# One pool of eight PSUM banks for scores and PV sums, with order rules chosen anew, in a fused attention and feed-forward kernel

## The chip, the cores and the metric

The kernel runs on one core of a Trainium2 chip. The metric is the device time of one execution in microseconds (us). Most executions agree within 0.3%. An execution can also fall into a slower state, with a lower granted clock; one did (experiment 10), and it is left out: fast executions are compared with fast ones only.

## The reference

```
xn  = layernorm(x)                         # x: 1 x 2048 x 640, bfloat16
q   = xn @ wq  -> 32 heads of 20           # wq: 640 x 640
k, v = xn @ wk, xn @ wv                    # ONE head of keys and values, 20 wide
p   = softmax(q k^T / sqrt(20))            # 32 heads x 2048 x 2048
att = (p v) @ wo
h   = relu(xn @ w1 + b1) ** 2              # 640 -> 1536
out = x + att + h @ w2 + b2
```

The scores are 2048 tiles of 128 keys x 512 queries. Each needs an exponential and a product with the values; the rest is small beside that.

## The kernel before

The program is not written as a fixed order. A list scheduler in it plans all instructions with modelled durations, picks a PSUM bank for each product, and then emits one instruction list per engine. What matters here:

- **Two ways for a tile.** ScalarE takes exponentials of two or three neighbouring banks at once (1480 tiles). VectorE and GpSimd replace the exponential of the other 568 by an approximation: four tiles (one VectorE score *set*) are evicted by VectorE as integers, then shifted in three *passes*.
- **Blocks.** 32 blocks of four heads x 512 queries. All PV products of a block (values times probabilities) add up in one bank. Then VectorE copies the sum out.
- **Banks.** PSUM is the memory that TensorE's products land in; the program has it as eight banks of 512 columns. A product is *evicted* when another engine copies it out. Seven banks are a pool for scores and dense products; the eighth belongs to the PV sums.
- **Start.** Rows are normalised, transposed and projected in four quarters. Scores of a quarter of keys can begin when that quarter has left PSUM (`KTe`).
- **Rules.** A table gives the scheduler other priorities in each stretch of 10 us of its plan.

```python
NB = 7          # pool: banks 0 to 6
PVB = 7         # the PV sums' own bank
RULES = {3: {'PVA': 2.1, 'PVD': 2.1, 'R3': 1, 'PP': 0.9}, ...}     # ... cut
ACTST = (2, 5, 6)             # rows with statistics on ScalarE

def make_step():                                   # scores for one exponential
    ...
    st_of = {bk: bank_state(bk) for bk in range(NB)}
    ...                                            # three neighbours, or the pair that is free first
        can = sorted((max(st_of[bk], st_of[bk + 1], t0), bk) for bk in range(NB - 1)
                     if st_of[bk] is not None and st_of[bk + 1] is not None)

def make_pv(b, kt):                                # PV products of block b
    first, last = b not in pv_begun, pv_count[b] == KT - 1
    ...
        parts.append(mm(ps[32 * h:32 * h + 32, PVB, :], vx[:, kt, :], PT[:, sl, :], first, last, (0, 32 * h)))
    if first and b > 0:
        deps.append(tn_op[b - 1])                  # wait until the old sum has been copied

def warm_parts():                                  # filler at the start
    return [lambda e: e.matmul(ps[:, PVB, :], ones_bf[:, :], hT_tmp[:, 0, :], start=True, stop=True)]

def odma(st, evs):                                 # store of a finished row block, by SyncE
    dma_out[st] = op(f"OD{st}", "SP", 0.45, lambda e: e.dma_start(out[0, st * 128:(st + 1) * 128, :], orow(st)), evs, ...)
```

The softmax here doesn't subtract the row's maximum and nothing guards it: scores larger than these inputs give would overflow.

## Time and profile before

| | before |
|---|---|
| time | 705.43 us, median of 3 (705.3 to 706.33) |
| profiled run | 705.39 us, span 703.6 |
| busy: TensorE, ScalarE, VectorE, GpSimd | 99%, 98%, 92%, 61% |
| exponentials that ScalarE issues | 715 (1480 tiles) |
| exponential that waits for the third quarter of keys | 32.44 us |
| last exponential ends | 695.14 us |
| last copy out by VectorE ends | 701.17 us |

The prediction below shows how the page, the chain and the start are read. Two more places also belong here. The first is the fourth quarter of keys, in VectorE's timeline (columns: start, length of the group, engine, line, operation, output and input, count, and in brackets the idle time before it and what ended it):

```profile
35.13 0.75 DVE L554 TENSOR_SCALAR kT<-ps,nk 128x512 bf16<-128x512 f32 x1 [1.80 <-PE ps L367]
```

The second is SyncE's issue of the four output stores at the end. Three issues take 1.30 us in all, and the last one is made 0.16 us after VectorE's last copy (701.17):

```profile
699.98 1.30 SPq L708 DMA_DIRECT2D out_dram<-out_sb  x3
701.33 0.45 SPq L708 DMA_DIRECT2D out_dram<-PT  x1
```

### The profile page before, as it was taken

How to read it: one execution, taken by the hardware profiler on the slowest of the kernel's cores; microseconds unless marked ns; L12 is line 12 of the kernel's file. 1: busy time of each engine (PE TensorE's matmuls, PEld its weight loads, DVE VectorE, ACT ScalarE, POOL GpSimd, SP SyncE). 2: the span in 40 equal slices, each digit the busy share in tenths (PEclk: the TensorE clock that was granted, in tenths of full speed). 3: DMA queues.
4: the chain of work that ended last, by engine and by line, in shares of the span. 5: the costliest groups of instructions: out<-in, count | busy, mean ns of one | idle time of the engine just before them, and what ended most of it. 6: DMA issues, size and time to landing. Idle time of an engine off the chain costs nothing.

```text
span 703.6 us, 22608 instructions
## 1 busy us (share of the span) xinstructions
PE 695.0 (99%) x9780; PEld 216.0 (31%) x9781; DVE 645.9 (92%) x1125; ACT 687.5 (98%) x739; POOL 427.3 (61%) x268
## 2 busy tenths in 40 slices
PE   8999999999999999999999999999999999999997
PEld 4422223233322223332322222323333222233333
DVE  7789999999999998989998998899899999999894
ACT  6899999999999999999999999999999999999995
POOL 4767556567566764666568765766665675644253
PEclk9999999999999999999999999999999999999999
DMA  6325422233337701211101001111112100031201
GB/s 201 98 70 153 115 78 58 81 97 80 84 85 160 162 20 25 55 40 37 52 18 40 23 22 28 29 47 26 46 42 51 36 22 23 20 106 51 55 26 39
DMA packets 42016, 44.00 MB, mean 63 GB/s; under 512 B 15540, under 2 KB 32772, under 8 KB 41788
## 3 DMA queue, kind: packets, MB, share of 16 engines
q1 hardware_dynamic: 39132, 36.93, 19.2%
q0 software_dynamic: 2208, 5.25, 3.9%
q8 instruction: 76, 1.25, 0.7%
q10 hardware_dynamic: 576, 0.38, 0.2%
q14 instruction: 24, 0.20, 0.1%
HBM read 28.03 MB, written 14.91 MB: 61 GB/s over the span
## 4 chain that ended last, share of the span: by engine, by line
ACT 95%; PE 4%; DMA 1%; DVE 0%; SPq 0%; issue 0%; DVEq 0%
ACT PT L910 94%; PE ps L367 3%; DMA x_sb<-in_A_x_dram 1%; PE ps L540 1%; ACT xnT L477 0%; ACT OC L421 0%; DVE out_sb L1164 0%; PE ps L568 0%; SPq L384 0%; ACT OC L422 0%; SPq L391 0%; PE ps L510 0%; PE ps L496 0%; DVEq L227 0%; DVE PT L1164 0%
## 5 line engine op out<-in xcount | busy, mean ns | idle before, releaser
L910 ACT ACTIVATE PT<-ps 128x1024 bf16<-128x1024 f32 (+1 forms) x715 | 677.1, 1219 | 3.8 <-PE ps L367 3.8
L1083 DVE TENSOR_SCALAR tmore<-ps 128x512 uint16<-128x512 f32 x568 | 367.4, 683 | 31.7 <-PE ps L367 28.2
L1101 POOL TENSOR_SCALAR tmore<-tmore 128x2048 uint16<-128x2048 uint16 x109 | 206.4, 1900 | 171.1 <-PE ps L367 62.3
L367 PE MATMUL ps<-qT,kT 20*128 20x512 bf16 x2048 | 281.7, 384 | 1.9 <-ACT PT L910 0.8
L1101 POOL TENSOR_SCALAR x_sb<-tmore 128x2048 uint16<-128x2048 uint16 x100 | 189.3, 1902 | 79.4 <-DVE x_sb L1101 24.2
L367 PEld LDWEIGHTS ps<-qT,kT 20*128 20x128 bf16 x2048 | 71.6, 91 | 280.4 <-ACT PT L910 233.1
L367 PE MATMUL ps<-PT,vx 128*32 128x512 bf16 x1480 | 136.9, 386 | 0.2 <-ACT PT L910 0.2
L1101 DVE TENSOR_SCALAR x_sb<-tmore 128x2048 uint16<-128x2048 uint16 x135 | 96.1, 745 | 0.1
L367 PE MATMUL ps<-x_sb,vxs 128*32 128x512 bf16 x940 | 83.2, 382 | 0.0
L367 PE MATMUL ps<-xnT,w_sb 128*32 128x512 bf16 x960 | 77.2, 384 | 0.1
L367 PE MATMUL ps<-w_sb,big 128*32 128x320 bf16 x1536 | 74.5, 302 | 0.0
L367 PE MATMUL ps<-tmore,vxs 128*32 128x512 bf16 x764 | 69.6, 382 | 0.0
L1101 DVE TENSOR_SCALAR tmore<-tmore 128x2048 uint16<-128x2048 uint16 x82 | 61.5, 770 | 0.1
L367 PE MATMUL ps<-tmore,vx 128*32 128x512 bf16 x568 | 55.7, 382 | 0.0
L367 PEld LDWEIGHTS ps<-PT,vx 128*32 128x32 bf16 x1480 | 34.9, 94 | 62.1 <-issue 53.6
L367 PEld LDWEIGHTS ps<-w_sb,big 128*32 128x32 bf16 x1536 | 32.1, 95 | 29.3 <-issue 22.2
L648 DVE TENSOR_SCALAR hT_tmp<-ps,b1col 128x512 bf16<-128x512 f32 x48 | 35.8, 746 | 3.4 <-PE ps L367 2.7
L367 PE MATMUL ps<-xnT,wq_sb 128*32 128x512 bf16 (+1 forms) x480 | 33.7, 356 | 0.2 <-DVE tmore L1083 0.2
L367 PE MATMUL ps<-wo_c,OC 128*32 128x320 bf16 x608 | 30.9, 301 | 0.0
L367 PEld LDWEIGHTS ps<-x_sb,vxs 128*32 128x32 bf16 x940 | 21.3, 95 | 19.9 <-issue 13.4
L367 PEld LDWEIGHTS ps<-xnT,w_sb 128*32 128x32 bf16 x960 | 17.6, 94 | 26.7 <-issue 22.4
L367 PEld LDWEIGHTS ps<-tmore,vxs 128*32 128x32 bf16 x764 | 18.1, 95 | 16.4 <-issue 11.5
(81 smaller groups left out, 259.4 us busy)
## 6 DMA issues: line engine op xcount, KB each, us to landing
xbd<-b2d SPq DMA_DIRECT2D x16, 320.0 KB, 4.4
xbd<-in_A_x_dram POOLq DMA_DIRECT2D x8, 640.0 KB, 5.8
xr<-xbd SPq DMA_DIRECT2D x32, 160.0 KB, 2.4
w_sb<-in_B_w_dram SPq DMA_DIRECT2D x8, 480.0 KB, 4.4
big<-OR SPq DMA_DIRECT2D x71, 40.0 KB
big<-drs SPq DMA_DIRECT2D x71, 40.0 KB
out_dram<-out_sb SPq DMA_DIRECT2D x15, 160.0 KB, 1.8
qT<-QCr SPq DMA_DIRECT2D x108, 20.0 KB
```

The costliest lines, as they stand in the source:

```text
L367: return lambda e: e.matmul(out_, l, r, start=start, stop=stop, tile_position=tp)
L540: return [(lambda e, dt=dt: e.transpose(out=psbf(bk)[:, dt * 128:(dt + 1) * 128], in_=xn_sb[:, st, dt:D:DT], identity=ident[:])) for dt in ...
L648: o = Op(f"RL{qc}_{f}", "DVE", 0.66, [lambda e: e.tensor_scalar(out=hT_tmp[:, k % 2, :], in0=ps[:, bk, :], scalar1=b1col[:, f:f + 1], scal ...
L910: return Op(f"ACT{st_['j']}", "ACT", 0.05 + 0.4267 * n, [lambda e: e.activation(out=PT[:, s0:s0 + n, :], in_=ps[:, b0:b0 + (n - 1) * db + ...
L1083: d1 = op(f"D1_{n}_{i}", "DVE", 0.60, lambda e: e.tensor_scalar(out=L[:, cs].bitcast(U16), in0=ps[:, bank, :], scalar1=XA, scalar2=XB, op0 ...
L1101: p = op(f"P{j}_{n}", eng, 0.60 if eng == "DVE" else 1.86, lambda e, T=T, j=j, two=two: e.tensor_scalar(out=T.bitcast(U16), in0=L.bitcast( ...
```

## The change

The intent: let the PV sum take any free bank. The next block's sum can then begin while VectorE still has to copy the old one, and the scores can use the eighth bank when it is free. The order rules were chosen again for this scheduler, with more weight on VectorE score sets early in each stretch.

```diff
-NB = 7
-PVB = 7
+NB = 8
+PV0 = 7
-RULES = {3: {'PVA': 2.1, 'PVD': 2.1, 'R3': 1, 'PP': 0.9}, ...      (the whole table, 51 entries: cut)
+DJIT = 9.0
+RULES = {3: {'D1P': 0.5, 'R3': 1}, 4: {'BEHIND': -0.1, 'PVA': 2.1}, ...      (cut)
-QEACT = (0, 1, 2, 3)
+QEACT = (0, 1)                       # two of four query evictions go to VectorE
-ACTST = (2, 5, 6)
-POOLXN = (2, 7, 9, 10, 11, 13, 14, 15)
+ACTST = (0, 2, 4)
+POOLXN = (7, 9, 10, 11, 13, 14, 15)
 ...                                   # PRIO, NBEF and FFN0 have other values too: cut
 def make_step():
-            st_of = {bk: bank_state(bk) for bk in range(NB)}
+            keep = kept()             # one bank is kept for a sum about to begin
+            st_of = {bk: bank_state(bk) if bk != keep else None for bk in range(NB)}
 ...
+        def bank_for(b):
+            if b in pv_bank:
+                return pv_bank[b]
+            can = [(bank_state(bk), -bk) for bk in range(NB) if bank_state(bk) is not None and ...]
+            return -min(can)[1] if can else None
 ...
 def make_pv(b, kt):
-                parts.append(mm(ps[32 * h:32 * h + 32, PVB, :], ...))
-            if first and b > 0:
-                deps.append(tn_op[b - 1])
+                parts.append(mm(ps[32 * h:32 * h + 32, bank, :], ...))
+            if first:
+                deps.append(bank_rel[bank])
 ...
 def make_dqk(heads):                  # scores for VectorE
+            if max(free["DVE"], free["PE"]) + sum(...) > free["PE"] + 0.43 + par("DJIT"):
+                return None
```

More of the change, by code (lines that the diff above doesn't have):

```diff
@@ L80 @@
 KEEP = 1
-RULES = {3: {'PVA': 2.1, 'PVD': 2.1, 'R3': 1, 'PP': 0.9},
-         4: {'PVA': 2.1, 'PVD': 2.1, 'R3': 1, 'PP': 0.9, 'WARM': 0.78},
-         5: {'D1P': 1, 'MPRIO': 0.5, 'PBIAS': 2.5},
-         6: {'D1P': 1, 'MPRIO': 0.5, 'PBIAS': 2.5, 'ND': 1, 'QKP': 0},
-         7: {'DQP': 2.05, 'URG': 2, 'PVD': 2.1, 'BEHIND': -0.3},
-         8: {'WARM': 0.85, 'DQP': 0.95},
-         10: {'ND': 1, 'NOPEN': 3},
-         11: {'ND': 1, 'NOPEN': 3},
-         12: {'EPS': 0.12},
-         13: {'EPS': 0.06, 'EVP': 0.3},
-         15: {'PBIAS': 0},
-         17: {'EPS': 0.06},
-         18: {'EPS': 0.12},
-         19: {'WARM': 0.78, 'PBIAS': 2.5, 'IDLE': 0.3},
-         21: {'PBIAS': 0, 'KEEP': 0},
-         23: {'EPS': 0.12},
-         25: {'R3': 1, 'EVP': 0.3},
-         26: {'R3': 1, 'EVP': 0.3, 'IDLE': 0.3, 'PVD': 2.1},
-         28: {'EPS': 0.12, 'URG': 3},
-         29: {'EPS': 0.12, 'URG': 3, 'KEEP': 3, 'EVP': 1.1, 'ND': 3},
-         31: {'PBIAS': 1, 'D1P': 1, 'PVD': 1.05},
-         32: {'PBIAS': 1, 'D1P': 1, 'PVD': 1.05, 'DGAP': 0.8, 'DQP': 0.95, 'SQP': 2, 'R3': 1},
-         36: {'PP': 0.9, 'BEHIND': -0.1, 'EVP': 0.3, 'PBIAS': 1.5},
-         37: {'URG': 3, 'JIT': 1.0, 'PVD': 1},
-         38: {'SQP': 0.7, 'URG': 3},
-         39: {'PP': 2.5},
-         40: {'PBIAS': 1},
-         41: {'PBIAS': 1, 'DGAP': 1.5, 'SQP': 0.7},
-         42: {'PBIAS': 1, 'DGAP': 1.5, 'SQP': 2, 'NOPEN': 3, 'ND': 2, 'PVD': 1},
-         43: {'PBIAS': 1, 'DGAP': 1.5, 'SQP': 2, 'NOPEN': 3, 'ND': 2, 'PVD': 1, 'R3': 9},
-         44: {'WARM': 0.78, 'KEEP': 3, 'DLAST': 7.5},
-         45: {'DGAP': 0.8, 'KEEP': 1, 'D1P': 3},
-         48: {'PBIAS': 1},
-         49: {'PBIAS': 1, 'R3': 1},
-         50: {'PBIAS': 1, 'R3': 1},
-         53: {'DLAST': 3.5},
-         54: {'DLAST': 3.5, 'EPS': 0, 'EVP': 0.3},
-         55: {'DLAST': 3.5, 'EPS': 0, 'EVP': 0.3, 'ND': 1},
-         56: {'EVP': 2, 'MPRIO': 1.0},
-         57: {'R3': 1, 'ND': 1},
-         58: {'BEHIND': -0.1, 'EPS': 0, 'PP': 4, 'R3': 1},
-         59: {'BEHIND': -0.1, 'EPS': 0, 'PP': 4, 'R3': 1, 'DRATE': 0.95, 'DLAST': 10, 'PVA': 2.1},
-         60: {'EVP': 1.1},
-         61: {'EVP': 1.1, 'SQP': 0.7},
-         62: {'EVP': 1.1, 'SQP': 0.7, 'KEEP': 3, 'R3': 1, 'NOPEN': 2, 'D1P': 3},
-         64: {'PP': 0.9, 'DRATE': 0.8},
-         65: {'R3': 1},
-         66: {'R3': 1},
-         67: {'EPS': 0.12, 'PVA': 1.05},
-         68: {'R3': 0},
-         69: {'R3': 0, 'JIT': 1.1}}
@@ new lines @@
+DJIT = 9.0
+RULES = {3: {'D1P': 0.5, 'R3': 1},
+         4: {'BEHIND': -0.1, 'PVA': 2.1},
+         6: {'EPS': 0.06},
+         7: {'EPS': 0.06, 'D1P': 0.5, 'KEEP': 1},
+         9: {'PBIAS': 1, 'PVA': 1, 'IDLE': 0.2, 'EPS': 0},
+         10: {'PBIAS': 1, 'PVA': 1, 'IDLE': 0.2, 'EPS': 0, 'ND': 1, 'NOPEN': 3},
+         11: {'IDLE': 2, 'EPS': 0.06},
+         13: {'URG': 3, 'KEEP': 3, 'NOPEN': 2, 'MPRIO': 0.9},
+         14: {'DRATE': 0.95, 'PBIAS': 0},
+         15: {'EPS': 0},
+         16: {'EPS': 0, 'KEEP': 0, 'DJIT': 9, 'PBIAS': 2.5},
+         17: {'MPRIO': 0.9, 'ND': 1},
+         18: {'MPRIO': 0.9, 'ND': 1, 'PBIAS': 1.5},
+         19: {'DLAST': 3.5, 'D1P': 3},
+         20: {'DLAST': 3.5, 'D1P': 3, 'PP': 2.5, 'PVD': 1.05},
+         21: {'DLAST': 3.5, 'D1P': 3, 'PP': 2.5, 'PVD': 1.05, 'DJIT': 0.6},
+         22: {'PP': 2.5, 'SQP': 0.7, 'BEHIND': 0.25},
+         23: {'PP': 2.5, 'SQP': 1.5, 'BEHIND': 0.25},
+         26: {'PVD': 2.1, 'EVP': 2, 'BEHIND': -0.1, 'DQP': 0.95},
+         27: {'QKP': 0, 'JIT': 1.1},
+         28: {'QKP': 0, 'JIT': 1.1, 'EVP': 2, 'R3': 0},
+         30: {'MPRIO': 1.0},
+         31: {'D1P': 0.5},
+         32: {'D1P': 0.5, 'DRATE': 1.1},
+         35: {'PP': 2.5, 'JIT': 0.9},
+         36: {'PP': 2.5, 'JIT': 0.9, 'DGAP': 0.8, 'URG': 3},
+         37: {'PBIAS': 1},
+         38: {'PBIAS': 1},
+         39: {'PBIAS': 1, 'MPRIO': 0.9, 'KEEP': 2, 'EPS': 0.06},
+         40: {'PBIAS': 1, 'MPRIO': 0.9, 'KEEP': 2, 'EPS': 0.06, 'R3': 0},
+         42: {'D1P': 3},
+         43: {'DJIT': 1.0, 'EVP': 0.3, 'PBIAS': 2.5},
+         44: {'URG': 4, 'PVA': 1.05, 'JIT': 0.82},
+         45: {'URG': 4, 'PVA': 1, 'JIT': 0.82, 'R3': 1, 'DLAST': 10, 'PBIAS': 2.5},
+         46: {'URG': 4, 'PVA': 1, 'JIT': 1.1, 'R3': 1, 'DLAST': 10, 'PBIAS': 2.5, 'EVP': 0.8, 'ND': 1, 'SQP': 0.7},
+         47: {'URG': 4, 'PVA': 1, 'JIT': 1.1, 'R3': 1, 'DLAST': 10, 'PBIAS': 2.5, 'EVP': 0.8, 'ND': 1, 'SQP': 0.7, 'DJIT': 0.6, 'EPS': 0.06},
+         51: {'QKP': 0, 'KEEP': 3},
+         52: {'DRATE': 0.95, 'PP': 4, 'MPRIO': 1.0, 'R3': 1},
+         54: {'PBIAS': 1.5, 'JIT': 1.0, 'IDLE': 0.1},
+         55: {'PBIAS': 1.5, 'JIT': 1.0, 'IDLE': 0.1, 'URG': 4, 'D1P': 0.5, 'EPS': 0.06},
+         56: {'PVA': 1.05, 'PBIAS': 0.6},
+         57: {'PBIAS': 1, 'DGAP': 1.5, 'KEEP': 2},
+         58: {'PBIAS': 0, 'DGAP': 1.5, 'KEEP': 2, 'R3': 1},
+         59: {'DRATE': 1.1},
+         60: {'DRATE': 1.1, 'PP': 2.5},
+         62: {'IDLE': 2, 'R3': 0},
+         63: {'PVD': 2.1},
+         64: {'JIT': 0.9, 'PBIAS': 0.6, 'SQP': 1.5, 'R3': 0},
+         65: {'PBIAS': 1.5},
+         66: {'PBIAS': 1.5, 'PP': 4, 'DQP': 2.05, 'SQP': 0.7, 'R3': 0},
+         68: {'EVP': 0.3, 'PVA': 1.05},
+         69: {'R3': 1}}
@@ L132 @@
 HOOK = None
-PRIO = {'NM15': 2.12, 'NM10': 2.88, 'PW2': 0.96}
-NBEF = {'AG4': 10.21, 'NM7': 11.5, 'Qe0_1': 10.11, 'PW12': 25.33}
+PRIO = {'XN1': 0.13}
+NBEF = {'S4a': 6.0, 'AG5': 10.23, 'PW1': 4.94}
 XACT = (1, 3)
-QEACT = (0, 1, 2, 3)
+QEACT = (0, 1)
 STOP = None
@@ L143 @@
 EARLYK = "F"
-FFN0 = 0.3
+FFN0 = 0.6
 OUT0 = 0.5
@@ L159 @@
 DEFAULTS = dict(EVP=EVP, PBIAS=PBIAS, MPRIO=MPRIO, DGAP=DGAP, DLAST=DLAST, DRATE=DRATE, BEHIND=BEHIND, IDLE=IDLE, URG=URG, NOPEN=NOPEN,
-                EPS=0.03, JIT=JIT, R3=R3, STATIC=STATIC, PVA=1, PVD=1, D1P=1, PP=4, SQP=2, DQP=3, QKP=0, ND=2, WARM=WARM, KEEP=KEEP)
+                EPS=0.03, JIT=JIT, R3=R3, STATIC=STATIC, PVA=1, PVD=1, D1P=1, PP=4, SQP=2, DQP=3, QKP=0, ND=2, WARM=WARM, KEEP=KEEP, DJIT=DJIT)
 class Ctr:
@@ L506, in fill_parts @@
         def fill_parts():
-            return [mm(ps[32 * jj:32 * jj + 32, PVB, :], zeros32[:, :], kT[:, 0:512], False, False, (0, 32 * jj)) for jj in range(4)]
+            return [mm(ps[32 * jj:32 * jj + 32, pv_bank[pv_blk[0]], :], zeros32[:, :], kT[:, 0:512], False, False, (0, 32 * jj)) for jj in range(4)]
         def warm_parts():
-            return [lambda e: e.matmul(ps[:, PVB, :], ones_bf[:, :], hT_tmp[:, 0, :], start=True, stop=True)]
+            return [lambda e: e.matmul(ps[:, PV0, :], ones_bf[:, :], hT_tmp[:, 0, :], start=True, stop=True)]
         def need_te(sts):
@@ L920, in after_act, with kept, pv_begin @@
                     pv_ready[key[0]].append(("A", key[1]))
+        pv_bank = {0: PV0}
+        bank_busy[PV0] = True
+        def bank_for(b):
+            if b in pv_bank:
+                return pv_bank[b]
+            can = [(bank_state(bk), -bk) for bk in range(NB) if bank_state(bk) is not None and not (par("STATIC") and bk in HELD)]
+            return -min(can)[1] if can else None
+        def kept():
+            b = pv_blk[0]
+            return bank_for(b) if b < NBLK and b not in pv_begun else None
+        def pv_begin(b):
+            if b not in pv_begun:
+                pv_bank[b] = bank_for(b)
+                bank_busy[pv_bank[b]] = True
+                pv_begun.add(b)
         def make_pv(b, kt):
@@ L924, in make_pv @@
             parts, deps = [], []
+            bank = bank_for(b)
             for h in range(HPG):
@@ L927, in make_pv @@
                 deps.append(o)
-                parts.append(mm(ps[32 * h:32 * h + 32, PVB, :], vx[:, kt, :], PT[:, sl, :], first, last, (0, 32 * h)))
+                parts.append(mm(ps[32 * h:32 * h + 32, bank, :], vx[:, kt, :], PT[:, sl, :], first, last, (0, 32 * h)))
             deps.append(v_op[kt // 4])
-            if first and b > 0:
-                deps.append(tn_op[b - 1])
+            if first:
+                deps.append(bank_rel[bank])
             return Op(f"PV{b}_{kt}", "PE", 0.222, parts, deps)
@@ L939, in make_dpv @@
             parts = []
+            bank = bank_for(b)
             for h in range(HPG):
                 i = s["order"].index(h)
-                parts.append(mm(ps[32 * h:32 * h + 32, PVB, :], wgt[:, kt, :], src[:, i * 512:(i + 1) * 512], first, last, (0, 32 * h)))
+                parts.append(mm(ps[32 * h:32 * h + 32, bank, :], wgt[:, kt, :], src[:, i * 512:(i + 1) * 512], first, last, (0, 32 * h)))
             deps.append(v_op[kt // 4])
@@ L945, in make_dpv @@
                 deps.append(vs_op[kt // 4][term - 1])
-            if first and b > 0:
-                deps.append(tn_op[b - 1])
+            if first:
+                deps.append(bank_rel[bank])
             return Op(f"DPV{b}_{kt}_{term}", "PE", 0.2205, parts, deps)
@@ L966, in emit_norm @@
             a = b % NOR
+            pb = pv_bank[b]
             if b >= NBLK - 2:
                 Tn, T2 = OR[:, a, :], QCr[:, 0, :]
-                tn = op(f"TN{b}", "DVE", 0.63, lambda e: e.transpose(out=Tn, in_=ps[:, PVB, :]), [lastpv] + or_users[a], prio=0)
+                tn = op(f"TN{b}", "DVE", 0.63, lambda e: e.transpose(out=Tn, in_=ps[:, pb, :]), [lastpv] + or_users[a], prio=0)
+                tn.frees = pb
                 rc = op(f"RC{b}", "DVE", 0.155, lambda e: e.reciprocal(out=Tn[:, DH:512:32], in_=Tn[:, DH:512:32]), [tn], prio=0)
@@ L977, in emit_norm @@
                 return
-            tn = op(f"TN{b}", "DVE", 0.60, lambda e: e.tensor_copy(out=OR[:, a, :], in_=ps[:, PVB, :]), [lastpv] + or_users[a], prio=0)
+            tn = op(f"TN{b}", "DVE", 0.60, lambda e: e.tensor_copy(out=OR[:, a, :], in_=ps[:, pb, :]), [lastpv] + or_users[a], prio=0)
+            tn.frees = pb
             tn_op[b] = tn
@@ L1041, in pool_banks @@
         def pool_banks():
+            keep = kept()
             if par("STATIC"):
-                return [bk for bk in POOLED if bk not in HELD and bank_state(bk) is not None]
-            fb = [bk for bk in POOLED if bank_state(bk) is not None]
+                return [bk for bk in POOLED if bk not in HELD and bk != keep and bank_state(bk) is not None]
+            fb = [bk for bk in POOLED if bk != keep and bank_state(bk) is not None]
             return fb if len(fb) > par("KEEP") else []
@@ L1055, in make_dqk @@
             if not fb or (len(fb) == 1 and behind()):
+                return None
+            if max(free["DVE"], free["PE"]) + sum(o.dur for o in dve_q if o.frees is not None) > free["PE"] + 0.43 + par("DJIT"):
                 return None
@@ L1119, in tail_bank @@
             bs = [bk for bk in range(NB) if (bk not in HELD or done) and bank_state(bk) is not None]
-            if tn_op.get(NBLK - 1) is not None and tn_op[NBLK - 1].fin is not None and not bank_busy[PVB]:
-                bank_rel[PVB] = bank_rel[PVB] or tn_op[NBLK - 1]
-                bs.append(PVB)
             return min(bs, key=lambda bk: (bank_state(bk), bk)) if bs else None
@@ L1229, in bass_parallel_sum__grouped_kv_mqa__dense_activation_squared_relu__prompt_kernel @@
             b = pv_blk[0]
-            if b < NBLK and (b == 0 or b - 1 in tn_op):
+            if b < NBLK and (b == 0 or b - 1 in tn_op) and bank_for(b) is not None:
                 for k, (kind, x) in enumerate(pv_ready[b]):
@@ L1324, in bass_parallel_sum__grouped_kv_mqa__dense_activation_squared_relu__prompt_kernel @@
             elif kind == "pv":
-                pv_begun.add(ap[1])
+                pv_begin(ap[1])
                 pv_of[(ap[1], pv_ready[ap[1]].pop(ap[2])[1])] = o
@@ L1328, in bass_parallel_sum__grouped_kv_mqa__dense_activation_squared_relu__prompt_kernel @@
             elif kind == "dpv":
-                pv_begun.add(ap[1])
+                pv_begin(ap[1])
                 s_, term = ap[3], ap[4]
```

## The prediction

> **What bounds the kernel now.** I read the page first (busy shares, chain of waits, costliest groups), then ScalarE's waits, then the chain in order of time, then the timelines of the first 35 us and the last 18 us.
>
> The page, parts 1, 4 and 5:
>
> ```profile
> PE 695.0 (99%) x9780; PEld 216.0 (31%) x9781; DVE 645.9 (92%) x1125; ACT 687.5 (98%) x739; POOL 427.3 (61%) x268
> ...
> ACT 95%; PE 4%; DMA 1%; DVE 0%; SPq 0%; issue 0%; DVEq 0%
> ...
> L910 ACT ACTIVATE PT<-ps 128x1024 bf16<-128x1024 f32 (+1 forms) x715 | 677.1, 1219 | 3.8 <-PE ps L367 3.8
> L1083 DVE TENSOR_SCALAR tmore<-ps 128x512 uint16<-128x512 f32 x568 | 367.4, 683 | 31.7 <-PE ps L367 28.2
> ```
>
> TensorE's 99% is a modelled pipeline and does not make it the bound; the chain line decides: 95% of the span is ScalarE taking exponentials (line 910), and these 715 instructions waited 3.8 us in all. There are 2048 score tiles of 128x512: ScalarE does 1480 of them, VectorE and GpSimd replace the exponential by an approximation on the other 568.
>
> ScalarE's timeline of the start, its groups by form, and the chain in order of time:
>
> ```profile
> 15.30 12.46 ACT L910 ACTIVATE PT<-ps 128x1024 bf16<-128x1024 f32 x13 [1.05 <-PE ps L367]
> 28.15 1.94 ACT L910 ACTIVATE PT<-ps 128x1024 bf16<-128x1024 f32 x2 [0.39 <-PE ps L367]
> 32.44 1.45 ACT L910 ACTIVATE PT<-ps 128x1536 bf16<-128x1536 f32 x1 [2.35 <-PE ps L367]
> ```
>
> ```profile
> L910 ACT ACTIVATE PT<-ps 128x1024 bf16<-128x1024 f32 x665 | 621.9, 1190 | 1.4 <-PE ps L367 1.4
> L910 ACT ACTIVATE PT<-ps 128x1536 bf16<-128x1536 f32 x50 | 79.0, 1609 | 2.3 <-PE ps L367 2.3
> ```
>
> ```profile
> 32.44 661.79 ACT PT L910 x699
> 694.23 0.04 issue
> 694.27 3.90 PE ps L367 x104
> 698.18 0.89 PE ps L367 x20
> 699.07 0.03 issue
> 699.10 1.28 DVE out_sb L1164 x3
> 700.37 0.40 DVE PT L1164
> ```
>
> So the time has three parts: a start up to 32.44 us, in which 15 instructions (31 tiles) were already done; an unbroken run of exponentials, 661.79 us, with no wait in it; and a tail of 703.6 - 694.23 = 9.4 us. The reported 705.43 us is 1.83 us above the profiled span of 703.6; I keep that offset.
>
> What held the step at 32.44 is seen on VectorE: the third quarter of the keys leaves PSUM there, and waited 1.58 us for TensorE.
>
> ```profile
> 30.94 0.75 DVE L554 TENSOR_SCALAR kT<-ps,nk 128x512 bf16<-128x512 f32 x1 [1.58 <-PE ps L367]
> ```
>
> **What the Trainium skill says.** "ScalarE: Activation LUTs", section "What ACT_TABLE_LOAD costs": one element per cycle and lane, 0.833 ns per element, for every function, and back-to-back ACTIVATEs overlap. The trace agrees nearly: 1609 - 1190 = 419 ns for 512 more columns, 0.818 ns each, and instructions follow each other faster than 1190 ns. No choice of PSUM bank changes the time that ScalarE needs per tile. "PSUM — Partial Sum Buffer", section "The four PSUM rules": a matmul output is at most one bank, of which there are eight. The kernel before gives seven to scores and other products and one for good to the PV sums; there is no ninth to gain. "GPSIMD Engine Reference", "1. Specifications": GpSimd shares its SBUF interfaces with VectorE, which matters as passes move to it; the trace has 1900 ns per pass on GpSimd against 745 to 770 on VectorE, but doesn't say how much of this is contention.
>
> **The change part by part.** I compared the two instruction orders and counted.
>
> Unchanged counts: 568 VectorE score tiles, so 1480 ScalarE tiles; 938 groups of four PV matmuls; all projections. "More weight on VectorE score sets" hence moves no tile off ScalarE. This is the main finding: the bound's work stays.
>
> 1. Width of the exponentials: 665 of two tiles and 50 of three become 674 and 44. From the run before: 715 - 15 = 700 instructions (the chain lists 699), 49 of them wide, in 661.79 us; with 0.419 us extra per wide one, the pace of a narrow one is (661.79 - 49 x 0.419) / 700 = 0.916 us, a wide one 1.335. In the new order the wait for the third quarter of keys falls after 32 tiles (13 narrow, 2 wide). Left then: 661 x 0.916 + 42 x 1.335 = 661.6 us. Against 661.8 that is nothing.
>
> 2. The start. Rows 0, 2, 4 instead of 2, 5, 6 get their statistics on ScalarE, and two of four query evacuations go to VectorE. Before, two transposes (13.99 to 14.87) stood ahead of the first scores on TensorE; in the new order they stand behind. Following the new order by hand with durations of this trace: ScalarE starts statistics at 4.2, is at row 4 when its data arrive (7.88), moves rows 1 and 3 until 9.85, finishes row 4 at 10.6, moves rows 0 and 2 until 11.8; TensorE then needs about 2 us for the last projections, two warming matmuls and two key groups; first exponentials at about 14.4 instead of 15.30. For the wait after 32 tiles I count VectorE work from 7.88 to the end of the third key evacuation: the order before has 21.1 us of it, and took 23.7; the new one has 21.7, but the last transposed row it needs comes 11 instructions earlier, so the 1.58 us wait should mostly go. That gives 29.5 plus 0.5 to 1.5 of waits, 30.0 to 31.0 for the end of the evacuation against 31.61, and the gated exponential about 0.9 later on account of what stands between on TensorE: about 31.3, with 32 tiles done. Gain: 32.44 - 31.3 = 1.1 us, and the tile more (0.43 us), which is already in item 1.
>
> 3. The pool of eight. PV sums may now start in another bank before the old sum is copied out (a copy lasts 0.68 us, 30 of these). It removes a wait on TensorE, but TensorE waited just 1.9 us in all for its score matmuls, and ScalarE not at all after 32.44. Worth nothing on the path. TensorE's work stays: 714 groups of score matmuls become 717, twelve more fillers.
>
> 4. Passes: 217 on VectorE and 209 on GpSimd become 204 and 222. VectorE loses about 13 x 0.7 = 9 us of its 646, GpSimd gains 13 x 1.9 = 25 us of 427. Both have room (92% and 61%), so none of it is on the path.
>
> 5. The tail. Before, seven of the eight half rows had a bank and were nearly summed when the last sum arrived, leaving 56 matmuls (32, 16 and 8). In the new order 84 are left (20, then 64 for three half rows), at 0.034 us each. The last half row is then ready about 2.9 us after the last transposed sum, and its copy out takes 0.4, while the chain before needed 3.0 in all, with VectorE's copies as the limit. Estimate: 0.5 us longer, 9.9.
>
> Sum: 31.3 + 661.6 + 9.9 = 702.8; with the offset of 1.83, 704.6. I allow 0.1 for a rare wait: 704.7.
>
> **The rivals.** (a) New waits in the long run. The run before had none in 661.8 us, so it can only get worse; the rules are tuned to modelled durations, and the accumulator competing with scores for banks could delay a step. If ten or so steps each lose 0.2 us, the time is 706.5 to 707. Against it: ScalarE runs at 100% in every window of 40 us that I looked at, with TensorE ahead of it. (b) The bank pool as a true gain: if the private PV bank had cost time, ScalarE would show waits during the run. It shows none, so the gain that could be had is bounded by start and tail, 3.8 + 1.05 us of start waits at most: about 701. (c) VectorE becomes the bound, since score sets start earlier: its waits for TensorE of 28.2 us speak against it, and it has fewer passes. It would show as 708 or more. (d) GpSimd's longer list makes the last passes late: the last sum would wait, and the tail grow by a pass, 1.9 us.
>
> **Range and chances.** Start between 30.5 and 32.5, tail 9.4 to 10.8, waits in the run 0 to 2: 702.3 to 707.0 holds it eight times in ten. Two per cent is 14 us, more than start waits and tail together could give, so faster by over 2% has a chance of 0.01; slower would take a broken pace in the run, 0.015.
>
> **What would show it right or wrong.** The page after should again have ScalarE at about 95% of the chain, with 718 exponentials; the first at 14 to 15 us; the last wait for keys over before 32 us; then one unbroken piece of about 661.6 us; a tail of about 9.9. Wrong would be: several pieces of ScalarE in the chain with waits on TensorE or VectorE between them (a), or a start later than 32.4 us (item 2).

## The result

After: **707.82 us**, median of 4 (706.97 to 707.92); before in the same rounds and earlier 705.88 (705.3 to 706.61). The ratio is 1.0024, 95% interval 1.0007 to 1.0042: the same within 2%, but slower, and outside the range that was predicted. (Ratios here are the mean time of one kernel's fast runs over that of the other's of the same rounds, so not quite the ratio of the medians.) The profiled runs are 705.39 and 707.92, spans 703.6 and 706.2. Before's profiled run lies 0.5 us below its median, so 2.6 us between the spans stand for 1.9 between the medians.

The page after, busy times, chain by engine, and the exponentials:

```profile
PE 698.0 (99%) x9793; PEld 217.9 (31%) x9793; DVE 644.7 (91%) x1115; ACT 687.7 (97%) x740; POOL 451.8 (64%) x280
...
ACT 68%; PE 30%; DMA 1%; SPq 0%; DVE 0%; issue 0%
...
L913 ACT ACTIVATE PT<-ps 128x1024 bf16<-128x1024 f32 (+1 forms) x718 | 677.9, 1214 | 5.1 <-PE ps L369 5.0
```

ScalarE's share of the chain (the work that ended last, followed back from the end) fell from 95% to 68%. That does not mean that TensorE became the bound for 30% of the time: the chain passes over to TensorE wherever ScalarE waited once for it, and then follows TensorE's backlog. The waits of the exponentials say how much it was: 5.0 us against 3.8. Where they lie is seen in ScalarE's timeline:

```profile
14.92 7.44 ACT L913 ACTIVATE PT<-ps 128x1024 bf16<-128x1024 f32 x8 [1.97 <-PE ps L369]
...
31.60 2.37 ACT L913 ACTIVATE PT<-ps 128x1536 bf16<-128x1536 f32 x2 [0.83 <-PE ps L369]
34.14 4.69 ACT L913 ACTIVATE PT<-ps 128x1024 bf16<-128x1024 f32 x5 [0.18 <-PE ps L369]
39.55 388.35 ACT L913 ACTIVATE PT<-ps 128x1024 bf16<-128x1024 f32 x415 [0.71 <-PE ps L369]
428.45 267.50 ACT L913 ACTIVATE PT<-ps 128x1536 bf16<-128x1536 f32 x281 [0.55 <-PE ps L369]
```

A new row begins wherever ScalarE stood idle. Before had one piece from 32.44 to the end. After has three more waits behind 31.60: 0.18, 0.71 and 0.55 us.

**The start.** The exponential that waits for the third quarter of keys comes at 31.60 with 32 tiles done, before at 32.44 with 31. So after leads there by 0.84 us and a tile (0.45), 1.29 us. Then it loses it. 47 tiles are done at 39.55; before had 47 at 32.44 + 2 x 1.336 + 5 x 0.917 = 39.70, worked out from the order of its widths and the paces. A lead of 0.15 is left, and by the start times of the single exponentials none at 43.36. VectorE's timeline shows what became late: the fourth quarter of keys begins to leave PSUM at 37.99, in before at 35.13, although the third came earlier:

```profile
29.93 0.75 DVE L556 TENSOR_SCALAR kT<-ps,nk 128x512 bf16<-128x512 f32 x1 [0.26 <-PE ps L369]
37.99 0.75 DVE L556 TENSOR_SCALAR kT<-ps,nk 128x512 bf16<-128x512 f32 x1 [2.23 <-PE ps L369]
```

**The wait at 428.** TensorE's timeline, then VectorE's:

```profile
426.19 0.39 PE L369 MATMUL ps<-qT,kT 20*128 20x512 bf16 x3
...
426.74 0.69 PE L369 MATMUL ps<-PT,vx 128*32 128x512 bf16 x8
...
428.01 0.39 PE L369 MATMUL ps<-qT,kT 20*128 20x512 bf16 x4
```

```profile
426.97 0.75 DVE L650 TENSOR_SCALAR hT_tmp<-ps,b1col 128x512 bf16<-128x512 f32 x1
427.63 0.68 DVE L1006 COPY OR<-ps 128x512 f32<-128x512 f32 x1
```

Scores (`ps<-qT,kT`) come on TensorE at 426.19, and the next only at 428.01, in a bank that the exponential just ended (427.90) had held. In between TensorE ends the PV sum of one block and begins that of the next (426.74: eight matmuls, four of each). VectorE does the eviction of a dense product first and copies the old sum out at 427.63. By the program's bank assignment the eight banks were then: two under the running exponential, two with VectorE score tiles, one with the dense product, the old sum, the new sum, and one single free bank. The new sum had taken one of the pair that the exponential before had released, so no pair was left for scores.

**The tail.** The chain in order of time, SyncE's issues, and the instruction fetch (DMA view of the half microsecond from 701.5; columns: packets, MB, share of 16 engines' time):

```profile
699.17 3.07 PE ps L369 x84
...
702.25 0.49 DVE PT L1193
```

```profile
700.96 2.74 SPq L710 DMA_DIRECT2D out_dram<-out_sb  x3
703.74 0.43 SPq L710 DMA_DIRECT2D out_dram<-PT  x1
```

```profile
q8 instruction: 1, 0.02, 19.1%
```

84 matmuls follow the last transposed sum, and VectorE's last copy ends at 702.74. But SyncE issues the last store only at 703.74, 1.0 us later (before: 0.16), because its third issue took 1.86 us instead of 0.4. Just there one packet of instructions for TensorE is loaded: 19.1% of 16 engines x 0.5 us is 1.53 us of one DMA engine. The Trainium skill, "Runtime: NRT & Kernel Launch", section "Instruction fetch mechanics", says that instructions are refilled in 16 KiB blocks of 256 over a DMA queue that the sequencer drives itself, and that crossing a boundary is "mostly hidden". The block size agrees: two fetches of after, at 697.2 and 701.8, lie 128 matmuls apart, and each matmul is two instructions (weight load and matmul). Hidden it was not here, if the two belong together, which the experiments had to show.

Where 2.60 us between the spans arise, by the ends of the same three events:

| | before | after | difference |
|---|---|---|---|
| exponential behind the third quarter starts | 32.44 | 31.60 | -0.84 |
| from there to the last exponential's end | 662.70 | 664.35 | +1.65 |
| to the end of the last transposed sum | 2.99 | 3.16 | +0.17 |
| to the end of VectorE's last copy | 3.04 | 3.63 | +0.59 |
| to the end of the span | 2.43 | 3.46 | +1.03 |

How far may single profiled runs be trusted here? Over three profiled runs with before's order (before and experiments 5 and 6), the second row read 662.70, 662.68 and 662.68; over four with after's (after and experiments 1, 2 and 4), 664.35, 664.35, 664.36 and 664.36. The first row scatters with the landing of the first rows of x: 32.00 to 32.67 and 31.18 to 31.60 in the same runs.

### The profile page after: what moved, and what is told of

It reads as the page before. It is cut to its first block, busy times and chain, and to the rows that moved or that the text cites. A ratio compares the mean times of both kernels' runs of the same rounds, so it can differ in the third digit from the quotient of the medians.

```text
span 706.2 us, 22591 instructions
## 1 busy us (share of the span) xinstructions
PE 698.0 (99%) x9793; PEld 217.9 (31%) x9793; DVE 644.7 (91%) x1115; ACT 687.7 (97%) x740; POOL 451.8 (64%) x280
## 4 chain that ended last, share of the span: by engine, by line
ACT 68%; PE 30%; DMA 1%; SPq 0%; DVE 0%; issue 0%
ACT PT L913 68%; PE ps L369 29%; DMA x_sb<-in_A_x_dram 1%; PE ps L542 1%; PE ps L570 0%; PE ps L512 0%; PE ps L498 0%; SPq L386 0%; ACT OC L423 0%; PE ps L477 0%; SPq L393 0%; ACT xnT L479 0%; DVE xnT L545 0%; DVE PT L1193 0%; PE ps L588 0%
## 5 line engine op out<-in xcount | busy, mean ns | idle before, releaser
L1133 POOL TENSOR_SCALAR tmore<-tmore 128x2048 uint16<-128x2048 uint16 x113 | 213.7, 1901 | 117.7 <-PE ps L369 37.0
L1133 POOL TENSOR_SCALAR x_sb<-tmore 128x2048 uint16<-128x2048 uint16 x109 | 206.1, 1902 | 104.2 <-DVE x_sb L1133 38.9
L1133 DVE TENSOR_SCALAR x_sb<-tmore 128x2048 uint16<-128x2048 uint16 x126 | 92.3, 754 | 0.0
L369 PE MATMUL ps<-x_sb,vxs 128*32 128x512 bf16 x940 | 86.1, 382 | 0.0
L1133 DVE TENSOR_SCALAR tmore<-tmore 128x2048 uint16<-128x2048 uint16 x78 | 58.9, 771 | 0.0
```

What stands on the lines that cost most here:

```text
L369: return lambda e: e.matmul(out_, l, r, start=start, stop=stop, tile_position=tp)
L1133: p = op(f"P{j}_{n}", eng, 0.60 if eng == "DVE" else 1.86, lambda e, T=T, j=j, two=two: e.tensor_scalar(out=T.bitcast(U16), in0=L.bitcast( ...
```

## The experiments

Ten kernels ran.

### 1. The last store from ScalarE's queue (actq)

```diff
-  dma_out[st] = op(f"OD{st}", "SP", ...
+  dma_out[st] = op(f"OD{st}", "ACT" if st == ST - 1 else "SP", ...
```

> The changed kernel, with only the store of the last row block issued by ScalarE's queue instead of SyncE's. Theory A (about 1 us of the 2 us loss is SyncE held up in the issue of the store before, 1864 ns instead of some 360, so that the last store starts 1.0 us after its data are ready): the last store starts within 0.3 us of VectorE's last copy, and the time falls by 0.6 to 0.9 us against the changed kernel (to about 707.0). Rival (the stores at the end are slow because of their own traffic, whoever issues them): the last store lands no earlier and the time stays at 707.8 within 0.2.

Measured: 707.43 us (707.33 to 708.36), ratio to before 1.0022 (1.001 to 1.0035). ScalarE issued the last store 0.03 us after VectorE's last copy, but SyncE's third issue was long again (1.56 us), and now that store landed last:

```profile
700.66 2.44 SPq L710 DMA_DIRECT2D out_dram<-out_sb  x3
```

That is 0.4 us less than after's median, less than I had expected, and the ratios to before (1.0022 and 1.0024) do not tell the two apart. In the profiled runs it is 0.2 us: 3.25 us from the last copy to the end instead of 3.46. So the queue behind the long issue was only part of the loss; the long issue delays its own store as well.

### 2. Instruction blocks moved (shift)

The warming matmuls at the start are cut into four columns each. That adds 63 matmuls (9793 to 9856 on the page) in an idle stretch of TensorE and moves every border of an instruction block in the program.

```diff
-  return [lambda e: e.matmul(ps[:, PV0, :], ones_bf[:, :], hT_tmp[:, 0, :], start=True, stop=True)]
+  return [lambda e, q=q: e.matmul(ps[:, PV0, 128*q:128*q+128], ones_bf[:, :], hT_tmp[:, 0, 128*q:128*q+128], ...)
+          for q in range(4)]
```

> The changed kernel, with the warming matmuls of the start written as four of 128 columns instead of one of 512: some 126 TensorE instructions more, the same columns, nothing else moved. Theory A1 (SyncE's long issue comes from the fetch of a 16 KB block of TensorE's instructions, which in the trace falls into the same microsecond): the fetches move by half a block, so the long issue at 701.8 us disappears or moves, and the time falls by 0.6 to 1.0 us. Rival (the long issue has to do with the stores themselves): it stays at the same place, the third store of the tail takes over 1.5 us to issue, and the time stays at 707.8 within 0.3.

(The number of added instructions named there is that of matmuls and weight loads together.) Measured: 706.50 us (706.43 to 707.25), ratio 1.0008 (0.9996 to 1.0021): no longer different from before. All five runs lie below all five of actq and of start in the same rounds.

```profile
700.82 1.38 SPq L710 DMA_DIRECT2D out_dram<-out_sb  x3
702.64 0.33 SPq L710 DMA_DIRECT2D out_dram<-PT  x1
```

The block now came at 700.1 and was loaded by 701.1. All three issues took 1.38 us, and the last copy (702.61) to the end took 2.19 us. This run alone takes 1.3 of 2.6 us away, and nothing of banks or order was touched.

### 3. The fourth quarter of keys earlier (start)

TensorE's order near 35 us is changed after the planning: the matmuls of the fourth quarter of keys go ahead of one group of scores.

```diff
+  reorder("PE", ["QK20", "KT3.1", "KT3.2", "KT3.3", "KT3.4", "QK21", "V3.0", "QK22", "B1.0", "QC0_2.0", "QC0_2.1"])
```

> The changed kernel, with eleven TensorE operations of the start in another order: the products for the fourth quarter of the keys stand together, and the first scores that need them come before two query products and the bias transpose. Everything after stands as it was. Theory B (the lead of 1.3 us that the new start has at 31.6 us is lost to the wait for the fourth quarter of keys at 39.55 us, and the run after it would keep a lead): that wait shrinks from 0.71 to under 0.2 us, the exponential there starts about 0.6 us earlier, the last exponential ends 0.6 earlier, and the time falls by 0.5 to 0.7 us. Rival (the lead is given back to TensorE later, since it stands on the chain of waits for 30% of the span): the wait shrinks but the last exponential ends at 695.95 within 0.2 us, and the time stays within 0.2 us.

Measured: 708.08 us (707.52 to 708.38), ratio 1.0028 (1.0015 to 1.0041). The keys began to leave PSUM at 37.23 instead of 37.99 (0.3 us of it because the run started earlier), but the wait only shrank from 0.71 to 0.57. TensorE's timeline says why:

```profile
38.71 0.39 PE L369 MATMUL ps<-qT,kT 20*128 20x512 bf16 x2 [0.62 <-ACT PT L913]
```

These scores had their keys, and now stood waiting for banks that ScalarE had yet to release. Nothing was gained later: the last exponential ended at 695.99, as the rival had it, although the run led by 0.33 us at the third quarter (31.27). By the start times of the single exponentials, the next ones came 0.18, 0.16 and 0.24 us behind their pace up to 43.39 (in after one, 0.16 at 43.36). Counted from the third quarter, the last exponential even ended 0.37 us later than in after (664.72 against 664.35). So it is not the keys alone that hold this place; the theory that they do falls. Why the lead at the third quarter is always paid back by the fourth is only partly settled: that both the keys and the lack of a pair of banks hold it is what these timelines suggest, and not shown by a run that takes both away.

### 4. Fewer matmuls at the end (skip)

As actq, with 24 products with wo left out in the last row block. 128 output rows are wrong.

```diff
-  yield Op(f"OF{st}_{h}_{c}", "PE", 0.136, out_chunks(...)[0][1](), deps), p, x, bk
+  yield Op(f"OF{st}_{h}_{c}", "PE", 0.136, out_chunks(...)[0][1]() if st < ST - 1 or c not in (1, 2, 3) else [], deps), p, x, bk
```

> As actq, and in the last row block (two half rows) 24 of the output projection's matmuls are left out; the result is wrong on purpose in 128 of 2048 rows. Theory C (half rows that are begun late cost 0.6 us in the tail: 84 matmuls after the last transposed sum instead of 56): VectorE's last copy ends about 3.0 to 3.1 us after the last transpose instead of 3.6, and the time falls by a further 0.5 to 0.6 us against actq. Rival (the copies of VectorE and GpSimd or the stores set the tail's end, not TensorE): under 0.2 us against actq.

Measured: 706.11 us (705.96 to 706.37), ratio 1.0001 (0.9988 to 1.0015). From the last transposed sum to the last copy 3.05 us, in actq 3.64: the 0.59 us are those matmuls. The rest of the gain over actq fits the instruction block again: with 24 matmuls fewer the last one was fetched at 696.64, none came among the stores, and three issues took 1.36 us.

### 5. and 6. The same block in the program of before (bnine, beighteen)

If the place of a block decides, before must be able to lose too. Its last block came at 695.89 with 116 matmuls left by the trace (the expectation says about 128), so the next, some 128 matmuls on, would have begun behind its end. After has 12 matmuls more, all fillers (9793 weight loads against 9781; one matmul of before has no record).

```diff
+  warm_n[0] += 1
+  if warm_n[0] > 3:                 # 6 in beighteen
       return [lambda e: e.matmul(ps[:, PVB, :], ...)]
+  return [... four columns of 128, as in shift ...]
```

> The kernel before, with the first three warming matmuls at the start cut into four columns each: 9 more matmuls in an idle stretch of TensorE, everything else as it was. In the trace of before, TensorE's last 16 KB instruction block is fetched at 695.85 us, with about 128 matmuls (256 instructions) left; so nothing more is fetched before its end. Nine more matmuls move every block border nine matmuls forward: one more block should then be fetched about nine matmuls before TensorE's end, near 700.0 us, where SyncE issues its stores (699.98 to 701.8). Theory A (the 1.03 us that after loses behind VectorE's last copy is the place of that fetch, set by a count of instructions that has nothing to do with banks or rules): one of SyncE's store issues becomes 1.3 us or more long, the stretch from VectorE's last copy to the end grows from 2.4 to 3.2 or more, and the time rises by 0.6 to 1.3 us to about 706.8. Rival (the long issue belongs to after's own order, for example to what else is in flight there): time within 0.3 us of before, all issues under 0.6 us. VectorE's last copy itself should end at 701.2 plus or minus 0.4 in both cases.

> As the run before it, but with six warming matmuls cut, 18 more matmuls: the extra block should be fetched about 18 matmuls before TensorE's end, near 699.6 us, some 0.4 us ahead of the first store issue and lasting 0.9 to 1.5 us by the records of the other runs. Theory A: it still overlaps the first issues; time 0.3 to 1.3 us above before, with one issue over 0.86 us. If the fetch ends before it can matter, time equals before within 0.3 us and the fetch shows earlier than the issues. Rival (not the fetch): the same as before in both runs, whatever the place of the fetch.

Measured: 705.09 us (704.9 to 705.6), ratio 0.999 (0.9979 to 1.0002), and 705.60 us (705.16 to 705.9), ratio 0.9995 (0.9983 to 1.0007); before 705.85 (704.79 to 707.18). The time did not rise. The traces do show the block and the longer issue, the line of the stores in each kernel (count: shortest, median and longest issue in ns), bnine first, beighteen second:

```profile
L713 SPq DMA_DIRECT2D out_dram<-out_sb x3: 332/430/880, 699.5 to 700.9; - x3
```

```profile
L713 SPq DMA_DIRECT2D out_dram<-out_sb x3: 332/430/624, 700.2 to 701.3; - x3
```

In bnine the block was loaded from 699.30 to 700.43. The first store issue, at 699.51, took its usual 0.33 us in spite of it; the second, from 699.94, took 0.88 and ended at 700.82. In beighteen the block was loaded from 699.65 to 700.86, and the second issue took 0.62 us and ended at 701.23. From the last copy to the end it took 2.99 and 2.72 us, in before 2.43. With the runs above there is a pattern: the long issue ended 0.37 to 0.40 us behind the end of the loading (after: 703.70 behind 703.33; actq: 703.10 behind 702.72; start, where it was the last store, 703.91 behind 703.51; bnine 0.39, beighteen 0.37).

The whole traces hold many more cases. In after 21 of SyncE's 600 issues took 0.86 us or more. All 21 overlap the loading of one of TensorE's blocks, and 20 of them ended 0.33 to 0.40 us behind its end; in before it is 14 of 14, and 13 of them ended 0.34 to 0.41 us behind it. The reverse does not hold: three issues of 0.29 to 0.32 us in after, from 199.25 on, began under a block that was loaded from 199.14 to 200.09. So an issue that is caught ends only some 0.4 us after the block is in, in before's program too; which issues are caught stays open.

Neither expectation came true as a whole. The issues were longer than the rival allowed in both runs, but the loss at the end, 0.56 and 0.29 us in these profiles, is not the 0.6 to 1.3 us that I expected, and it is less than the scatter of the start.

### 7. The wait at 428 alone (mid)

```diff
 def kept():
+    if stage[0] == 43 and b not in pv_begun and (b - 1 not in tn_op or tn_op[b - 1].fin is None):
+        return None                 # no bank kept before the old sum is copied
-if b < NBLK and (b == 0 or b - 1 in tn_op) and bank_for(b) is not None:
+if b < NBLK and (b == 0 or b - 1 in tn_op) and bank_for(b) is not None and (stage[0] != 43 or b in pv_begun or tn_op[b - 1].fin is not None):
+    if o.name == "RL1_9": o.nb = 421.5          # the dense eviction behind the copy
-PRIO = {'XN1': 0.13}
+PRIO = {'XN1': 0.13, 'TN18': 0.0}
```

> After, with one local change near 427 us, where ScalarE waited 0.55 us (428.45): at that change of blocks the new PV sum may take a bank only once the old sum has been copied out, and VectorE makes that copy ahead of one eviction of the dense part. The scores then get the pair of banks that the sum had taken. The instruction stream up to 426 us is the same; after it the rules meet another state, and as they were fitted to one schedule the end may be several us later; this run is for the stretch around 428 us only. Theory (a bank taken by the new sum while the old one waits for VectorE, rival a of the prediction): no wait over 0.1 us on ScalarE between 40 and 440 us, so one piece of exponentials from about 39.5 past 440, and at 440 us ScalarE stands 0.5 us ahead of after. Rival (TensorE has simply too much work there, and no bank is the cause): a wait of 0.4 to 0.8 us shows up again between 427 and 440. Whole time: 707 to 714, not judged.

```profile
39.14 576.44 ACT L915 ACTIVATE PT<-ps 128x1024 bf16<-128x1024 f32 x616 [0.71 <-PE ps L369]
616.16 71.95 ACT L915 ACTIVATE PT<-ps 128x1536 bf16<-128x1536 f32 x70 [0.58 <-PE ps L369]
```

The wait is gone: one piece from 39.14 to 615.58. At 440 us mid stood 1.1 us ahead of after, 0.4 of it from the start; 0.5 had been expected. So rival (a), the new sum's bank and the old sum's late copy together, made it; the edit changes both at once and does not part them. But the time was 711.27 us (one run, so its state is unknown; granted clock 1.0). Waits of 0.58 and 0.15 us came up elsewhere (616 and 688 us). The rules met another state behind 428 us, and the plan ended with 560 VectorE tiles instead of 568:

```profile
L1119 DVE TENSOR_SCALAR tmore<-ps 128x512 uint16<-128x512 f32 x560 | 363.3, 683 | 35.5 <-PE ps L369 32.3
```

Eight tiles more on ScalarE are about 8 x 0.45 = 3.6 us by the paces. The last exponential ended at 699.38, 3.4 us later than in after; counted from the exponential at 39 us, which mid reached 0.41 us earlier, it is 3.84. A wait of half a microsecond was removed at the price of two score sets.

### 8. and 9. The pool without rules (seven, eight)

Both have an empty table of rules and the start of before. Seven is otherwise before; eight has after's scheduler with its pool.

```diff
-RULES = {3: {...}, ...}
+RULES = {}
```

> The kernel before (seven banks and one for the PV sums, the start of before) with its table of order rules emptied, so that the list scheduler runs on its defaults. Counted in its instruction order: 140 VectorE score sets instead of 142 (560 tiles, so 1488 tiles for ScalarE). It is the baseline for the next run. From the run mid, which also has 560 tiles and ended its exponentials 3.4 us after those of after: 8 tiles at about 0.45 us are 3.6 us more on ScalarE, and unfitted rules should leave a few waits of 0.5 to 2 us in the run: 712 to 718 us.

> The run seven, with the pool of eight alone added (after's scheduler, the start and the empty rules of seven): also 140 sets, so ScalarE's work is the same. It asks what the shared banks are worth without rules fitted to either. Theory of the prediction (item 3: the private bank cost nothing on the path, so pooling gains nothing): last exponential within 1 us of seven's. Theory that the pool gains: ScalarE's waits in the run fall by more than 1 us. Theory that it costs (the sum competes with scores): they rise by more than 1 us. The tail is left to chance by both (84 matmuls or more after the last transposed sum are possible) and is judged apart: last exponential's end to the program's end.

Measured: seven 715.37 us (715.35 to 716.59), ratio 1.0135 (1.0119 to 1.0151); eight 719.89 us (719.82 to 720.08), ratio 1.0196 (1.0179 to 1.0213). Both have 560 VectorE tiles. ScalarE's timeline, seven first:

```profile
32.33 318.87 ACT L860 ACTIVATE PT<-ps 128x1536 bf16<-128x1536 f32 x342 [1.89 <-PE ps L317]
351.47 104.55 ACT L860 ACTIVATE PT<-ps 128x1024 bf16<-128x1024 f32 x113 [0.28 <-PE ps L317]
457.85 244.05 ACT L860 ACTIVATE PT<-ps 128x1024 bf16<-128x1024 f32 x261 [1.82 <-PE ps L317]
```

```profile
32.11 291.19 ACT L862 ACTIVATE PT<-ps 128x1536 bf16<-128x1536 f32 x316 [1.89 <-PE ps L318]
323.85 273.51 ACT L862 ACTIVATE PT<-ps 128x1024 bf16<-128x1024 f32 x295 [0.55 <-PE ps L318]
597.92 103.24 ACT L862 ACTIVATE PT<-ps 128x1536 bf16<-128x1536 f32 x110 [0.56 <-PE ps L318]
```

From the exponential at 32 us to the end of the last: 669.57 us in seven (701.90 - 32.33), 669.05 in eight (701.16 - 32.11). The pool alone is worth 0.5 us of the run: its waits are 1.0 us shorter (1.11 against 2.10), and 26 exponentials of three tiles became 16, which gives 0.4 back (15 narrow ones more x 0.917 less 10 wide ones x 1.336). Within the 1 us that was named before the run for the prediction's item 3. The 4.5 us that eight is slower come behind the last exponential: 16.6 us against 11.3, since TensorE still had a backlog of dense products there (546 matmuls in an unbroken row up to 715.1 in the chain).

### 10. Before's rules on the pool (swap)

```diff
 after's scheduler with
-RULES, PRIO, NBEF, QEACT, FFN0, ACTST, POOLXN of after
+RULES, PRIO, NBEF, QEACT, FFN0, ACTST, POOLXN of before
```

> After's scheduler (pool of eight) with the rules and the start of before: do the rules carry over? If the order rules were good in themselves, this would come within 2 us of before (706 to 708). If they are fitted to one schedule, which the pool changes from the first new sum on, it has fewer VectorE sets (139 counted in its order, so 12 tiles more for ScalarE, about 5.4 us) and new waits in the run of a few us: 714 to 720 us. The stretch up to the first exponentials after 32 us should be that of before to 0.5 us, and the run between its first 40 and 90 us without a wait.

Measured: 718.57 us (718.42 to 718.93 in three fast runs; a fourth, 732.7 at a granted clock of 0.979, is left out), ratio 1.0177 (1.016 to 1.0194). 556 VectorE tiles, 12 fewer than before. Its start is that of before, but 0.74 us later (33.18 against 32.44; 0.5 had been expected at most), by as much as one row of x landed later: its statistics began at 8.62 instead of 7.88. The first wait behind it comes at 93.2 us. So the pool alone does not make after's waits at 34 and 39.5 us (eight has none up to 323.30 either); they came with the new start and order. In swap, six waits of 5.6 us in all follow up to the end, that one included, the longest of 2.46 us at 674.32. The rules of before, worth 10 us with its own banks (715.37 against 705.9), are worth about 1 us with the pool (719.89 in eight against 718.57).

No version came out that beats both kernels: shift brought after level with before, bnine is not told apart from it, and a search for other rules by the planning durations had found nothing by then that promised more than 0.4 us.

## Why the prediction was wrong

Its centre was 704.7 us and its range ended at 707.0; the median is 707.82. Two steps failed: the unbroken run of exponentials, which was broken three times (1.85 us), and the end of the tail, where a step was missing (1.2 us). With the instruction block moved (shift, 706.50) the same order lies inside the range; that would have been luck, since the first step fails there as well. In spans, it expected 702.8, and 706.2 came. Its bound and most of its mechanism were right: the 568 VectorE tiles stayed, so ScalarE's work stayed, and the two kernels are equal within 0.3%. Its steps one by one:

- **Item 1, widths and pace: right.** 397 narrow and 18 wide exponentials from 39.55 on: 397 x 0.917 + 18 x 1.336 = 388.1 us; measured 388.35.
- **Item 2, the start: right up to where it looked.** The third quarter's eviction ended at 30.68, in the predicted 30.0 to 31.0 (that of before, by the line shown, at 31.69 and not 31.61). The exponential behind it came at 31.60 (31.33 in the mean of six runs with this start) against 31.3, with the 32 tiles counted; the very first at 14.92 against 14.4.
- **"Left then: 661 x 0.916 + 42 x 1.335 = 661.6", an unbroken run: this step failed, by 1.85 us.** That piece, measured as in the table, was 664.35 us where 662.5 followed from it. Three waits of 0.18, 0.71 and 0.55 us and their restarts (0.13 us each: the pieces are 0.39 us longer in sum than the paces give) make 1.83. (The prediction's 661.6 ends where the chain passes from ScalarE to TensorE, at 694.23 in before; the table's row ends 0.91 later, with the last exponential.) The first two come from a quarter of keys that I didn't follow: I worked the third quarter through the new order, and took over for the fourth that before had no wait for it. It began to leave PSUM 2.86 us later than in before. The lead (1.1 us and a tile predicted, 1.29 us measured) was right in kind, and worth 0.15 us fifteen tiles later.
- **Rival (a): right in kind, and given too little weight.** The sum competes with scores for banks, and mid shows that the wait at 428 was this. It came once in the long run, not ten times. The sign named for (a), ScalarE in several pieces with waits on TensorE between them, is what the page and timeline show. That ScalarE showed no wait in before spoke only for before's order.
- **Item 3, the pool is worth nothing on the path: right within its meaning.** Without rules it saved 0.5 us of the run.
- **Item 5, the tail: the counted part right, 1.2 us missing.** 84 against 56 matmuls: predicted 0.5, measured 0.59, and skip took just this away. Another 0.17 us came from PV products that were still queued behind the last exponential. And 1.03 us came from a place that is in no step: the issue of a store under the loading of an instruction block. shift takes 1.3 us away by moving the block; actq, bnine and beighteen show the same long issue in other places. That it could happen could have been seen before: before's trace has 14 such long issues, 116 matmuls were left at its last block, and twelve more were counted in the new order, 128 in all and so one block.
- **Item 4: counts right, size off, and off the path.** Passes are 204 and 222, and GpSimd gained 24 us. But VectorE's busy time fell by 1.2 us, not 9: its passes fell by 6.4, and other work grew, most of all the 19 products of the normalisation, from 14.2 to 17.4 us at the same number of elements. Neither engine bounds anything; rivals (b), (c) and (d) did not come. (The bound of (b), about 701, counts the 1.05 us of the first wait twice: the 3.8 us hold it already, so it is 701.6.)

The range was also too narrow for its own scatter: the first rows of x land up to 0.7 us apart from run to run, and before itself ran from 704.79 to 707.18.

What stays open: what holds the start between 34 and 43 us in the first place, since keys and banks seem to bind almost together; and why some store issues wait for a block to be loaded and others don't: the traces show that the long ones end just behind the loading, not what holds them.

## What to carry to other kernels

A gain at one gate is worth what the next gate lets through: follow the new order through every gate up to where the bound runs free, not only the one that showed the wait before. Shared buffers move a wait from one user to another, and order rules fitted to one plan are part of that plan: judge a pool with the rules taken out of both sides, and expect fitted rules to lose their worth when anything moves. When differences of 0.2% matter at the end of a kernel, look at the issue queue and the instruction blocks there, and try a shift of the program before believing a reason.

## What the Trainium skill lacked or had wrong

- "Runtime: NRT & Kernel Launch", "Instruction fetch mechanics": the block of 256 instructions agrees (128 matmuls with their weight loads between the last two fetches of after). "Mostly hidden" leaves out the other engines: a block was one packet of 0.88 to 1.52 us on one DMA engine in after, and one SyncE store issue made meanwhile took 0.62 to 1.86 us instead of 0.33 to 0.46 and ended 0.37 to 0.40 us behind the fetch (in after, actq, start, bnine and beighteen). Every SyncE issue of 0.86 us or more in after overlaps such a fetch (21 of 21), but not every issue under a fetch is long.
- "DMA: Bandwidth & Descriptors", "Issuing engines are not separate DMA queues": transfers of all engines run on the same 16 DMA engines, and issuing on several saves only issue time. actq agrees: the second queue gained 0.2 us of 1.0. The page doesn't count instruction fetches among the users of these engines.
- "ScalarE: Activation LUTs", "What ACT_TABLE_LOAD costs": 186 ns + 0.833 ns per element and 93 ns of overlap give an estimate of 946 ns from one 1024-element exponential to the next, if the scale and bias, which the program gives as numbers, count as immediate; the runs show 917 ns, and 0.818 ns per further element. The mean of 1190 ns that the profile's groups print is not the cost of one: 273 ns of it lie under the exponential ahead.
